# Keys' and queries' bf16 parts stored once in DRAM, repeated by the load

## The chip, the cores and the metric

The kernel runs on one core of a Trainium2 chip. A core has five engines that work side by side: TensorE (PE; its weight loads are listed as PEld), VectorE (DVE), ScalarE (ACT), GpSimd (POOL) and SyncE (SP), and 16 DMA engines. Every DMA but one of this kernel is issued by SP, one after the other; the row "SPq" of the profile is SP's queue. The metric is the time of one execution on the device in microseconds (us). The kernel before took 918.21 us, the median of three runs (917.14 to 920.17).

## The reference

One transformer block over 2,048 rows of width 512. A condition vector gives six modulation vectors. The rows are normalized and modulated, go through an attention with memory (32 heads of width 16, four segments of 512 rows), and then through a second normalization and a bilinear feed-forward layer of width 1,376.

```python
for s in range(N):
    qs, ks, vs = q[:, :, s], k[:, :, s], v[:, :, s]
    logits = jnp.einsum("bhqd,bhkd->bhqk", qs, ks) * scale + mask
    p = _softmax(logits, axis=-1)
    a_dot = jnp.einsum("bhqk,bhkd->bhqd", p, vs)
    pq = phi(qs)
    num = jnp.einsum("bhld,bhde->bhle", pq, M)
    den = jnp.einsum("bhld,bhd->bhl", pq, z)[..., None] + 1e-6
    o = g * (num / den) + (1.0 - g) * a_dot
    pk = phi(ks)
    M = M + jnp.einsum("bhld,bhle->bhde", pk, vs)
    z = z + jnp.einsum("bhld->bhd", pk)
```

The mask is added to the keys that lie before the query's row in the segment, so only keys from the same row back to the first take part. Softmax is of float32 precision, and the kernel keeps it by splitting numbers into parts.

## The kernel before

**Parts.** A float32 key or query is written as a sum of three bf16 numbers, part 0 the largest and part 2 the smallest. Of the nine products of parts, six are kept: 0·0, 0·1, 1·0, 0·2, 1·1 and 2·0. With heads of width 16, six products make a contraction of 6 x 16 = 96 rows, so one bf16 matmul over 96 partitions gives the logits. For that a key tile `kst` holds the parts of the keys in the order 0, 1, 2, 0, 1, 0 (16 partitions each), and a query tile `qst` those of the queries in the order 0, 0, 0, 1, 1, 2. Two more partitions (96 and 97) hold the negative row maximum in two parts and a row of ones, for the second matmul.

**From the projection to the tiles.** `a_kq` (L636) computes keys or queries of one group: eight heads of one segment (four segments, four groups, 16 in all). The projection lies in PSUM as 128 partitions (width times heads) by 512 rows. ScalarE copies it and rounds it to part 0; GpSimd subtracts; ScalarE rounds to part 1; GpSimd subtracts to part 2 (in the very first group VectorE stands in for GpSimd and for the second rounding). The three parts stand side by side in the tile `q3` (two buffers). Three transfers then write them to a DRAM tile of six slots, `kd` or `qd` (L664 and L667): for keys the slots 0 to 2 from parts 0 to 2, slots 3 and 4 from parts 0 and 1, slot 5 from part 0; for queries part 0 three times, part 1 twice, part 2 once. Each such transfer waits only for the parts it reads.

`load(u)` (L228) brings one unit, four heads of a group, from DRAM: one transfer of 96 partitions by 4 KB for keys and one for queries (L231). There are 32 units; four buffers of each tile.

**The loop.** Iteration v (L936) of 34 has five slots. In them unit v+1 or v+2 runs `q_step` (logits with queries as stationary operand; VectorE takes the row maximum), unit v runs `k_step` (L278; logits with keys as stationary operand, less the maximum, then exp on ScalarE and the causal triangle on GpSimd), and unit v-1 runs `av_step` (probabilities times values) and `t_step` (division, store). After slot 2, `n_step` (L268) of unit v+1 brings its row maxima across the partitions: a transpose on TensorE, a copy to `nt` on VectorE and two transfers of one row of 4 KB into partitions 96 and 97 of `qst` (L276), which `k_step` of the next iteration reads. In slot 1, once the projections of the group are done, `load(v+3)` is issued.

Between these steps the loop fills in other work by a fixed rate (`fill`, L868): projections of the next group and segment, the memory, and later the preparation of the feed-forward layer. The loads of units 0, 1 and 2 stand ahead of the loop (L917, L931 and L932). The order of TensorE's instructions is that of the program text; for the other queues, SP's among them, the framework's scheduler orders the instructions by a timeline of its own. SP executes its queue in order. Eight semaphores tell of landed DMAs; they are given out in turn, so that a DMA of SP also waits until the eighth before it has landed, where that isn't known already.

After the loop the feed-forward layer runs (L1002 on), for which keys and queries are no longer used.

Of the kernel before, what the change touches and what calls it, by code (L numbers as in the profile page):

```python
# [10 lines left out]
BF = mybir.dt.bfloat16  # L11
AF = mybir.ActivationFunctionType
# [5 lines left out]
P = 128  # L18
S, D, H, DH, NSEG, L, F = 2048, 512, 32, 16, 4, 512, 1376
KT = D // P  # L20
NG = 4
HG = 8
# [35 lines left out]
def tile_kernel(ctx, tc, x, wq, wk_, wv, wo, beta, w_gate, w_up, w_down, c, w_mod, out):  # L58
    nc = tc.nc
# [19 lines left out]
    def pin(i):  # L79

        if last_pe[0] is not None:
            tc.add_manual_dep(i.ins, last_pe[0].ins.name, NOSYNC, reason="order")

    def MM(*a, **k):
        return pe(nc.tensor.matmul(*a, **k))  # L85
# [4 lines left out]
    CV, CA = Chain(tc, nc.vector), Chain(tc, nc.scalar)  # L90
    vec, act = Switch(nc.vector), Switch(nc.scalar)
    cst = ctx.enter_context(tc.tile_pool(name="cst", bufs=1))
    wpool = ctx.enter_context(tc.tile_pool(name="wp", bufs=1))
    dram = ctx.enter_context(tc.tile_pool(name="dram", bufs=1, space=DRAM))
# [10 lines left out]
    def bank(name, dt=F32, shape=(P, 512)):  # L105

        nbank[0] += 1
        return pst(shape, btag[nbank[0] % len(btag)], name, dt)
# [20 lines left out]
    be = cst.tile([P, H], F32, name="be")  # L129
    e1 = cst.tile([P, KT], F32, name="e1")  # L130

    qd = [[dram.tile([6, P, L], BF, name=f"qd{s}_{g}") for g in range(NG)] for s in range(NSEG)]
    kd = [[dram.tile([6, P, L], BF, name=f"kd{s}_{g}") for g in range(NG)] for s in range(NSEG)]
    memd = [[dram.tile([P, 4 * HG * DH], F32, name=f"memd{s}_{g}") for g in range(NG)] for s in range(NSEG)]
    od = [dram.tile([4, P, D], F32, name=f"od{s}") for s in range(NSEG)]
    x1d = [[dram.tile([P, D], F32, name=f"x1d{s}_{t}") for t in range(4)] for s in range(NSEG)]
# [76 lines left out]
    HQ = 4  # L213
    NB = 4
    NQ = NSEG * NG * 2
    kst = [ap.tile([98, HQ, L], BF, name=f"kst{i}") for i in range(NB)]
    qst = [ap.tile([98, HQ, L], BF, name=f"qst{i}") for i in range(NB)]
# [9 lines left out]

    def load(u):  # L228
        s, g, j = u // 8, u // 2 % 4, u % 2
        for t, d in ((kst[u % NB], kd), (qst[u % NB], qd)):  # L230
            nc.sync.dma_start(t[0:96].rearrange("p h t -> p (h t)"),  # L231
                              d[s][g].rearrange("r (d h) t -> (r d) (h t)", h=HG)[:, j * HQ * L:(j + 1) * HQ * L])

    nms = {}

# [253 lines left out]
    r0 = [[a[:, j].rearrange("p i c -> p (i c)") for a in wm0] for j in range(2)]  # L489
# [139 lines left out]
    def flush():  # L629

        while later:
            later.pop(0)()
# [3 lines left out]
    def a_kq(s, g, nm):  # L636

        hH, hL = hcur[0]
        ph = phs.setdefault((s, g), {})
        if True:  # L640
            dst = kd if nm == "k" else qd
            ps = bank(f"{nm}ps{s}_{g}")
            n = 0
            for k in range(KT):
                for a, b in ((wH, hH), (wL, hH), (wH, hL)):
                    MM(ps, a[nm, g][:, k, :], b[k], start=n == 0, stop=n == 11)
                    n += 1
                    if n in (3, 6, 9):
                        yield 0.68
            f = pa.tile([P, L], F32, tag="f", name=f"{nm}f{s}_{g}", bufs=2)  # L650
            fast = s == 0 and g == 0
            A, V = (CA, CV) if fast else (act, nc.gpsimd)
            A.activation(f, ps, AF.Copy)
            q3 = pa.tile([P, 3, L], BF, tag="q3", name=f"{nm}3_{s}_{g}", bufs=2)
            r = pa.tile([P, L], F32, tag="qr", name=f"{nm}r_{s}_{g}", bufs=2)
            A.activation(q3[:, 0, :], f, AF.Copy)
            V.tensor_sub(r, f, q3[:, 0, :])

            def rest():
                (CV.tensor_copy if fast else act.copy)(q3[:, 1, :], r)  # L660
                V.tensor_sub(q3[:, 2, :], r, q3[:, 1, :])
                for r0, n, k in ((0, 3, 0), (3, 2, 0), (5, 1, 0)) if nm == "k" else ((0, 1, 3), (3, 1, 2), (5, 1, 1)):
                    if nm == "k":
                        nc.sync.dma_start(dst[s][g][r0:r0 + n].rearrange("r p t -> p r t"), q3[:, 0:n, :])  # L664
                    else:
                        i = 3 - k
                        nc.sync.dma_start(dst[s][g][r0:r0 + k].rearrange("r p t -> p r t"),  # L667
                                          q3[:, i:i + 1, :].to_broadcast([P, k, L]))

            if fast:  # L670
                rest()
            phi = (nm == "k" and s < NSEG - 1) or (nm == "q" and s > 0)
            if phi:
                if fast:
                    yield 0.0
                if nm == "q" and g > 0:
                    yield from drain()
                e = pa.tile([P, L], F32, tag="ph", name=f"ph{nm}{s}_{g}", bufs=3)
                rl = pa.tile([P, L], F32, tag="rl", name=f"rl{nm}{s}_{g}", bufs=1)
                act.activation(rl, f, AF.Relu)  # L680
                act.activation(e, f, AF.Exp)
                ph[nm] = e
            yield 0.68
            if not fast:
                rest()
            if phi:
                later.append(lambda: pin(vec.scalar_tensor_tensor(e, e, 1.0, rl, op0=ALU.min, op1=ALU.add)))
                if fast:
                    flush()
        nkq[s, g] = nkq.get((s, g), 0) + 1  # L690
        if nkq[s, g] == 2:
            done.add((s, g))
# [10 lines left out]
    def drain():  # L703
        while memq:
            w = mem_step()
            if w is not None:
                yield w
# [76 lines left out]
    def fill_a():  # L784
# [5 lines left out]
        for s in range(NSEG):  # L790
# [4 lines left out]
            for g in range(2 if s == 0 else 0, NG):  # L795
# [3 lines left out]
                for w in ws:  # L799
                    next(w)  # L800
                K, Q = a_kq(s, g, "k"), a_kq(s, g, "q")
                if g >= 2 and s + 1 < NSEG:
                    if g == 2:
# [101 lines left out]
    next(lw[2])  # L905
    next(lw[2])
    kq0 = [a_kq(0, 0, "k"), a_kq(0, 0, "q")]
    while next(kq0[0]) != 0.0:
        pass
# [5 lines left out]
    run(kq0[1])  # L915
    run(kq0[0])
    load(0)  # L917
    av = a_v(0)
    for i in range(5):
# [6 lines left out]
    for w in w2:  # L926
        next(w)
    run(a_kq(0, 1, "k"))
    run(a_kq(0, 1, "q"))
    flush()  # L930
    load(1)  # L931
    load(2)  # L932
    btag[:] = ["ms"]
    vec.eng = CV
    share = (0.25, 0.0, 0.25, 0.25, 0.25)
    for v in range(-2, NQ + 1):  # L936
        rate[0] = 5.5
        on, prev = 0 <= v < NQ, 0 <= v - 1 < NQ
        for slot in range(5):
            i = (slot + 3) % 5  # L940
            u = v + 2 if i < 3 else v + 1
# [54 lines left out]
    for s in range(NSEG):  # L996
# [30 lines left out]
        for i in range(NF):  # L1027
            if i + 1 < NF:
                gate_up(i + 1)
            n = ft[i][1]  # L1030
# [47 lines left out]
```

## Time and profile before

| what | value |
|---|---|
| median of three runs | 918.21 us (917.14 to 920.17) |
| the profiled execution | 917.86 us, its span 916.1 us |
| TensorE busy | 877.6 us, 96% of the span |
| VectorE, ScalarE, GpSimd busy | 534.9, 408.3, 315.5 us |
| DMA moved | 109.81 MB; HBM read 67.98 MB, written 40.63 MB |
| DMA queue of SP | 37.7% of 16 engines' span |

The span is the time from the first to the last instruction in the trace. Where the profile lists a group of instructions, the line number is that of the code (L85 is the helper for matmuls), then come engine, operation, and the tiles as "written<-read". A row of SPq shows the issue of a transfer, not its movement. "DMA to landing" is the time from that issue until the semaphore tells that all bytes have arrived. A wait is put down to what ended it last.

### The profile page before, as it was taken

Reading aid. Unit: us, or ns where it says so; the run is one execution under the profiler, and the core shown is the slowest. Engines: PE = TensorE matmul, PEld = TensorE weight load, DVE = VectorE, ACT = ScalarE, POOL = GpSimd, SP = SyncE. Lnnn points to the kernel's source line nnn. Section 1 sums busy time; section 2 is a strip of 40 time slices with the busy share of each in tenths; the row PEclk is TensorE's granted clock in tenths of the full one; section 3 lists DMA queues with packets and bytes.
Section 4 is the critical chain, followed back from the end, with each engine's and each line's share of the span. In section 5 each row is a group of like instructions: output and inputs, shape, how many; then the busy total and the mean of one; then the engine's idle time right before and its main releaser. Section 6 shows DMA issues by size and latency. Waiting matters only on the chain.

```text
span 916.1 us, 14191 instructions
## 1 busy us (share of the span) xinstructions
PE 877.6 (96%) x5083; PEld 623.1 (68%) x5084; DVE 534.9 (58%) x1587; ACT 408.3 (45%) x603; POOL 315.5 (34%) x460
## 2 busy tenths in 40 slices
PE   8988999999999899998998999999999999999998
PEld 4655656556656565565655678887888788878886
DVE  8688877897789977787886326553133213321112
ACT  3647767787577865675546412231112111211111
POOL 4435536565464762666424406540000000000000
PEclk9989999999999999998998999999999999999999
DMA  7773544664455544659551433331101110100011
GB/s 230 223 215 115 186 117 155 205 197 145 134 164 178 179 133 125 198 181 307 169 170 59 139 126 109 110 95 58 46 1 47 47 47 0 47 19 29 1 46 47
DMA packets 86215, 109.81 MB, mean 120 GB/s; under 512 B 9504, under 2 KB 58656, under 8 KB 86144
## 3 DMA queue, kind: packets, MB, share of 16 engines
q1 hardware_dynamic: 86000, 108.89, 37.7%
q8 instruction: 40, 0.66, 0.3%
q14 instruction: 31, 0.25, 0.1%
q10 hardware_dynamic: 144, 0.02, 0.0%
HBM read 67.98 MB, written 40.63 MB: 119 GB/s over the span
## 4 chain that ended last, share of the span: by engine, by line
PE 59%; DVE 5%; ACT 3%; issue 1%; DMA 1%; POOL 0%; DVEq 0%
PE gps L1014 13%; PE acc L1035 13%; PE ups L1014 13%; PE wops L85 4%; PE tb L85 3%; PE k L85 3%; DVE q L39 3%; PE q L85 2%; PE qps L85 1%; PE vps L85 1%; ACT pt L296 1%; PE kps L85 1%; PE ctp L88 1%; PE tr L88 1%; PE up L85 1%
## 5 line engine op out<-in xcount | busy, mean ns | idle before, releaser
L39 DVE CUSTOM_DVE_ANT_0 q<-q,cmask 128x384 f32<-128x384 f32 (+3 forms) x512 | 246.9, 508 | 53.0 <-PE q L85 42.6
L296 ACT ACTIVATE pt<-k 128x1024 f32<-128x1024 f32 x160 | 163.7, 1023 | 77.3 <-PE k L85 75.5
L299 POOL TENSOR_SCALAR_AFFINE_SELECT pt<-pt 128x256 f32<-128x256 f32 (+1 forms) x224 | 99.4, 457 | 174.2 <-ACT pt L296 172.0
L1019 DVE TENSOR_TENSOR gs<-gs,ups 128x512 f32<-128x512 f32 (+1 forms) x44 | 30.2, 687 | 194.9 <-PE ups L1014 194.9
L85 PE MATMUL q<-kst,qst 96*128 96x384 bf16 (+3 forms) x512 | 101.6, 303 | 7.7 <-DVE nm L39 5.5
L85 PE MATMUL k<-qst,kst 98*128 98x384 bf16 (+3 forms) x512 | 98.4, 305 | 10.6 <-ACT pt L296 8.0
L1018 ACT ACTIVATE gs<-gps 128x512 f32<-128x512 f32 (+1 forms) x44 | 26.2, 597 | 146.6 <-PE gps L1014 146.6
L1022 ACT ACTIVATE mH<-gs 128x512 fp32r<-128x512 f32 (+1 forms) x44 | 27.8, 633 | 130.2 <-DVE gs L1019 126.7
L85 PE MATMUL tb<-pt,v 128*32 128x512 f32 (+3 forms) x1024 | 76.7, 440 | 0.0
L85 PEld LDWEIGHTS <-kst 98*128 98x128 bf16 x512 | 38.8, 99 | 53.6 <-issue 44.2
L39 DVE DVE_READ_ACCUMULATOR2_ANT nm<- 128x1 f32 x512 | 72.6, 142 | 0.0
L1014 PE MATMUL gps<-chH,gL 128*128 128x512 f32 (+1 forms) x176 | 69.3, 394 | 0.0
L1014 PE MATMUL gps<-chH,gH 128*128 128x512 f32 (+1 forms) x176 | 69.3, 394 | 0.0
L1014 PE MATMUL ups<-chH,uH 128*128 128x512 f32 (+1 forms) x176 | 69.3, 394 | 0.0
L1035 PE MATMUL acc<-dH,mL 128*128 128x512 f32 (+1 forms) x176 | 69.3, 394 | 0.0
L1035 PE MATMUL acc<-dL,mH 128*128 128x512 f32 (+1 forms) x176 | 69.2, 393 | 0.0
L1014 PE MATMUL gps<-chL,gH 128*128 128x512 f32 (+1 forms) x176 | 69.2, 393 | 0.0
L1014 PE MATMUL ups<-chL,uH 128*128 128x512 f32 (+1 forms) x176 | 69.2, 393 | 0.0
L1014 PE MATMUL ups<-chH,uL 128*128 128x512 f32 (+1 forms) x176 | 69.2, 393 | 0.0
L85 PEld LDWEIGHTS <-qst 96*128 96x128 bf16 x512 | 43.6, 98 | 35.2 <-issue 10.1
L1035 PE MATMUL acc<-dH,mH 128*128 128x512 f32 (+1 forms) x176 | 65.0, 395 | 0.0
L85 PEld LDWEIGHTS tb<-pt,v 128*32 128x32 f32 x1024 | 28.7, 110 | 39.9 <-issue 34.5
(215 smaller groups left out, 1660.7 us busy)
## 6 DMA issues: line engine op xcount, KB each, us to landing
kst<-kd SPq DMA_DIRECT2D x32, 384.0 KB, 4.4
qst<-qd SPq DMA_DIRECT2D x32, 384.0 KB, 5.2
wm<-in_w_mod_dram SPq DMA_DIRECT2D x24, 256.0 KB, 5.4
kd<-k SPq DMA_DIRECT2D x16, 384.0 KB, 4.0
qd<-q SPq DMA_DIRECT2D x16, 384.0 KB, 2.9
x<-in_x_dram SPq DMA_DIRECT2D x16, 256.0 KB, 4.2
kd<-k SPq DMA_DIRECT2D x16, 256.0 KB, 3.2
qd<-q SPq DMA_DIRECT2D x16, 256.0 KB, 3.4
```

The costliest lines, as they stand in the source:

```text
L39: i = getattr(self.eng, name)(*a, **k)
L85: return pe(nc.tensor.matmul(*a, **k))
L88: return pe(nc.tensor.transpose(*a))
L296: act.activation(pt, kp, AF.Exp, scale=0.25)
L299: sels[u, i] = nc.gpsimd.affine_select(w, w, pattern=[[0, w.shape[1]], [1, P]], compare_op=ALU.is_ge, fill=0.0, base=0, channel_multiplier=-1)
L1014: nc.tensor.matmul(ps[0:n], a[:, k, 0:n], b[k], start=j == 0, stop=j == 11)
L1018: act.activation(gs[0:n], pss[0][0:n], AF.Copy)
L1019: vec.tensor_mul(gs[0:n], gs[0:n], pss[1][0:n])
L1022: act.activation(mH[0:n], gs[0:n], AF.Copy)
L1035: nc.tensor.matmul(acc[t], a[0:n, t * P:(t + 1) * P], b[0:n, :], start=i == 0 and j == 0, stop=i == NF - 1 and j == 2)
```

## The change

The DRAM tiles `kd` and `qd` have three slots instead of six. Keys are written in the order 0, 1, 2 and queries in the order 2, 1, 0 by one transfer each, once all three parts are there. The repetition moves to the load: each side of a unit is filled by three transfers of 48, 32 and 16 partitions. For keys these read the first 48, 32 and 16 rows of the DRAM tile (parts 0 1 2, 0 1 and 0); for queries the last 48, 32 and 16 rows (parts 2 1 0, 1 0 and 0). The pairs that meet in the contraction are now 0·2, 1·1, 2·0, 0·1, 1·0 and 0·0: the same six products in another order. Per group there are 2 writes and 12 load transfers, where there were 6 and 4.

```diff
-    qd = [[dram.tile([6, P, L], BF, name=f"qd{s}_{g}") for g in range(NG)] for s in range(NSEG)]
-    kd = [[dram.tile([6, P, L], BF, name=f"kd{s}_{g}") for g in range(NG)] for s in range(NSEG)]
+    qd = [[dram.tile([3, P, L], BF, name=f"qd{s}_{g}") for g in range(NG)] for s in range(NSEG)]
+    kd = [[dram.tile([3, P, L], BF, name=f"kd{s}_{g}") for g in range(NG)] for s in range(NSEG)]
...
     def load(u):
         s, g, j = u // 8, u // 2 % 4, u % 2
-        for t, d in ((kst[u % NB], kd), (qst[u % NB], qd)):
-            nc.sync.dma_start(t[0:96].rearrange("p h t -> p (h t)"),
-                              d[s][g].rearrange("r (d h) t -> (r d) (h t)", h=HG)[:, j * HQ * L:(j + 1) * HQ * L])
+        n = HQ * L
+        for t, d, q in ((kst[u % NB], kd, 0), (qst[u % NB], qd, 1)):
+            d = d[s][g].rearrange("r (d h) t -> (r d) (h t)", h=HG)
+            for r, m in ((0, 48), (48, 32), (80, 16)):
+                i = 48 - m if q else 0
+                nc.sync.dma_start(t[r:r + m].rearrange("p h t -> p (h t)"), d[i:i + m, j * n:(j + 1) * n])
...
-            A.activation(q3[:, 0, :], f, AF.Copy)
-            V.tensor_sub(r, f, q3[:, 0, :])
+            i0, i1, i2 = (0, 1, 2) if nm == "k" else (2, 1, 0)
+            A.activation(q3[:, i0, :], f, AF.Copy)
+            V.tensor_sub(r, f, q3[:, i0, :])
 
             def rest():
-                (CV.tensor_copy if fast else act.copy)(q3[:, 1, :], r)
-                V.tensor_sub(q3[:, 2, :], r, q3[:, 1, :])
-                for r0, n, k in ((0, 3, 0), (3, 2, 0), (5, 1, 0)) if nm == "k" else ((0, 1, 3), (3, 1, 2), (5, 1, 1)):
-                    if nm == "k":
-                        nc.sync.dma_start(dst[s][g][r0:r0 + n].rearrange("r p t -> p r t"), q3[:, 0:n, :])
-                    else:
-                        i = 3 - k
-                        nc.sync.dma_start(dst[s][g][r0:r0 + k].rearrange("r p t -> p r t"),
-                                          q3[:, i:i + 1, :].to_broadcast([P, k, L]))
+                (CV.tensor_copy if fast else act.copy)(q3[:, i1, :], r)
+                V.tensor_sub(q3[:, i2, :], r, q3[:, i1, :])
+                nc.sync.dma_start(dst[s][g].rearrange("r p t -> p r t"), q3)
```

## The prediction

> **What bounds the kernel now.** I read the page first, then the busy time by stage, the waits of TensorE, and at last the DMA queue and the tiles that the change touches.
>
> ```profile
> PE 877.6 (96%) x5083; PEld 623.1 (68%) x5084; DVE 534.9 (58%) x1587; ACT 408.3 (45%) x603; POOL 315.5 (34%) x460
> ...
> q1 hardware_dynamic: 86000, 108.89, 37.7%
> ```
>
> TensorE is busy for 96% of the span and the DMA engines for 38%. A change that only touches transfers can move the end only where TensorE stands still for a transfer. The stages (columns: window, length, busy time and count of each engine, granted clock, DMA share, GB/s) show where transfers are dense:
>
> ```profile
> 41.00:62.00 21.00, 17.19 (x86) 11.26 (x87) 18.16 (x67) 8.34 (x13) 7.46 (x6) 0.97 0.87 265
> 62.00:180.00 118.00, 114.18 (x810) 71.59 (x808) 95.73 (x337) 83.69 (x122) 62.19 (x95) 0.98 0.49 153
> 520.00:916.00 396.00, 390.31 (x1741) 313.67 (x1733) 123.81 (x202) 72.34 (x120) 43.12 (x44) 1.00 0.17 54
> ```
>
> From 41 to 62 us the DMA engines are 87% busy and TensorE is idle for 3.8 of 21 us. From 62 us on they are half busy, and after 520 us, where keys and queries are no longer touched, TensorE has the stage to itself. The waits of TensorE (total, times, longest) name the transfers:
>
> ```profile
> PE k L85 <- DMA qst<-nt: 2.6, 1, 2.6
> ...
> PE q L85 <- DMA qst<-qd: 1.0, 1, 1.0
> ```
>
> Only these two waits, 3.6 us together, hang on the tiles of the change, and both stand in the first 62 us:
>
> ```profile
> 58.18 0.39 PE L85 MATMUL qps<-ahL,wqH 128*128 128x512 f32 x1
> 61.18 1.03 PE L85 MATMUL k<-qst,kst 98*128 98x512 bf16 x2 [2.60 <-DMA qst<-nt]
> ```
>
> **The start, where it counts.** Unit 0's first k matmul (61.18) needs the two small rows of row maxima (L276). What stands ahead of them in the queue:
>
> ```profile
> 45.97 0.32 SPq L231 DMA_DIRECT2D kst<-kd  x1
> 46.38 0.38 SPq L667 DMA_DIRECT2D qd<-q  x1
> 46.81 0.43 SPq L588 DMA_DIRECT2D wrk<-in_wk_dram  x1
> 47.29 0.67 SPq L588 DMA_DIRECT2D wrq<-in_wq_dram  x1
> 48.01 0.98 SPq L464 DMA_DIRECT2D x<-in_x_dram  x2
> 49.30 0.33 SPq L231 DMA_DIRECT2D qst<-qd  x1
> 49.67 0.91 SPq L464 DMA_DIRECT2D x<-in_x_dram  x2
> 50.62 0.65 SPq L231 DMA_DIRECT2D kst<-kd  x1
> 51.32 0.51 SPq L231 DMA_DIRECT2D qst<-qd  x1
> 53.37 1.23 SPq L276 DMA_DIRECT2D qst<-nt  x2
> ```
>
> The landing times of the last three lines, each asked for alone, are 9.2, 9.5 and 7.1 to 7.6 us:
>
> ```profile
> DMA to landing us min/median/max: 9.2/9.2/9.2
> ...
> DMA to landing us min/median/max: 9.5/9.5/9.5
> ...
> DMA to landing us min/median/max: 7.1/7.4/7.6
> ```
>
> So the key load lands at 50.62 + 9.2 = 59.8, the query load at 60.8, the small rows at about 61.1: a train of transfers that ends at 61 us holds TensorE. Its bytes: four loads of 384 KB, six of 256 KB (weights and x), a 128 KB query write, together 3,200 KB. If its data begin about 0.9 us after the first issue (an estimate from the two ends of it), it runs at 3,200 KB in 13.9 us, 230 KB per us, close to the 252 GB/s of the stretch:
>
> ```profile
> 53.00:61.00 8.00, 5.53 (x29) 3.59 (x27) 7.75 (x30) 4.28 (x8) 4.51 (x4) 0.98 0.92 252
> ```
>
> **The change part by part.** *Writes.* Each group and side wrote 384 + 256 + 128 KB in three transfers and now writes 384 KB in one: 16 groups x 2 sides x 384 KB = 12.6 MB and 64 issues less. The three went out as their parts became ready; the one waits for the last part, which GpSimd makes (VectorE in the first group). For keys the last write was already the full 384 KB one, so nothing is later there; for queries the last was 128 KB. From the sizes:
>
> ```profile
> kd<-k SPq DMA_DIRECT2D x16, 384.0 KB, 4.0
> qd<-q SPq DMA_DIRECT2D x16, 384.0 KB, 2.9
> ...
> kd<-k SPq DMA_DIRECT2D x16, 128.0 KB, 3.3
> qd<-q SPq DMA_DIRECT2D x16, 128.0 KB, 3.8
> ```
>
> the median landing hardly depends on the size (2.9 to 4.0 us against 3.3 to 3.8), so the write costs -0.9 to +0.7 us per group, off the path.
>
> *Loads.* 64 transfers of 96 partitions (384 KB) become 192 of 48, 32 and 16 partitions (192, 128, 64 KB): the same bytes, 128 more issues; with the writes 64 more in all. SP spends 0.3 to 0.65 us on one (rows above), 0.4 taken: 2 x 0.4 = 0.8 us more per load of a side, 64 x 0.4 = 26 us more on SP over 460 us. What takes the cover in the long stage is time: load(v+3) goes out in slot 1 of one iteration and is used in slot 2 of the next. An iteration is 124.67 - 111.46 = 13.2 us by the issues of the small rows:
>
> ```profile
> 111.46 1.15 SPq L276 DMA_DIRECT2D qst<-nt  x2
> ...
> 124.67 1.15 SPq L276 DMA_DIRECT2D qst<-nt  x2
> ```
>
> ```profile
> kst<-kd SPq DMA_DIRECT2D x32, 384.0 KB, 4.4
> qst<-qd SPq DMA_DIRECT2D x32, 384.0 KB, 5.2
> ...
> qst<-nt SPq DMA_DIRECT2D x64, 4.0 KB, 1.7
> ```
>
> ```profile
> 118.08 0.61 PE L85 MATMUL k<-qst,kst 98*128 98x512 bf16 x2
> ```
>
> A load that lands after 5.2 us has over 8 us to spare; 2 x 0.8 us do not reach TensorE. I take 0; if the loads used up all of that, each further us would be paid in up to 30 units. Behind the loads on SP stand the small rows: issued at 111.46 + 1.15, landed 1.7 us later, used at 118.08, they have some 4 us to spare. SP gives each DMA one of eight semaphores in turn, so a DMA also waits until the eighth before it has landed; a unit's six loads fill most of these. In an iteration the loads leave in slot 1 and the small rows after slot 2, so I take 0 here too.
>
> *Reads of the loaded tiles.* In the changed program's instruction list TensorE, VectorE, ScalarE and GpSimd have the same instructions in the same order; only SP's queue differs. TensorE's first q matmul of a unit waits for three transfers a side, 83 waits more in all. [...] ScalarE and GpSimd wait for one write instead of three before a buffer of parts is used again: 0 to a gain.
>
> *The sum at the start.* Keys' last part of group 1 was issued at 40.74 and landed 5.2 us later behind two other key writes and two query writes; alone I take 3.0 (the 384 KB write of group 0 at 27.1 us):
>
> ```profile
> DMA to landing us min/median/max: 3.0/3.0/3.0
> ...
> DMA to landing us min/median/max: 5.2/5.2/5.2
> ```
>
> ```profile
> 43.73 1.17 POOL L661 TENSOR_TENSOR q<-qr,q 128x512 bf16<-128x512 f32 x1 [1.92 <-ACT q L660]
> ```
>
> So the train starts at 43.7 rather than 45.97, the query write at 44.9 rather than 46.38, with 256 KB more in it: 3,456 / 230 = 15.0 us from 44.6 on, to 59.6, and the small rows at 59.8, 1.4 us earlier. SP's 12 load issues in the train instead of four and the wait for the eighth before take back some; 0.4 taken. The first q matmul (1.0 us of waiting now) moves by -1.0 to +0.6: the query write is three times as large, the load three issues long, the traffic beside it less. It is swallowed by the later wait, since TensorE waits at 58.6 anyway. **Sum: -1.0 us.** The gain ends at -3.6, where both waits are gone. On the other side stands the train slowed by its smaller loads, below.
>
> **The trace's own time** is 917.86 us (span 916.1 and 1.8 around it), 0.35 below the median 918.21. 917.86 - 1.0 = 916.9; against the median 917.2 us.
>
> [...]
>
> **Rivals.** *1, slower: narrow loads move at half speed.* Place: the train. Its last two 384 KB loads land 1.0 us apart (59.8, 60.8), so a side would take 1.0 us more; four sides make +4.0: small rows at 60.2 + 4.0 = 64.2, 3.0 after the 61.2 of before: 921.2. It turns to a loss of over 0.3% from 0.95 us per side on. For it: three transfers share what one had; against: neighbouring transfers overlap in the queue, and 252 GB/s is well below the 314 that the writes reach at 41 to 46 us:
>
> ```profile
> 41.00:46.00 5.00, 4.66 (x22) 3.14 (x23) 3.85 (x15) 1.10 (x2) 1.99 (x2) 1.00 0.90 314
> ```
>
> *2, faster: the writes' time comes back in full* and both waits vanish: 918.2 - 3.6 = 914.6. Against it: the loads, weights and x in the train stay as they are.
>
> *3, slower: SP becomes the bound.* The small rows stand behind six loads and the wait for the eighth before; once they are 4 us late, every further 0.3 us costs 30 x 0.3 = 9 us: 927. The only unit with no room to spare now is that at 281.37, where the rows follow a query load that waited for its write:
>
> ```profile
> 280.96 0.32 SPq L231 DMA_DIRECT2D qst<-qd  x1
> 281.37 1.15 SPq L276 DMA_DIRECT2D qst<-nt  x2
> ```
>
> There two issues more cost 0.8 and the shorter writes give about as much.
>
> [...]
>
> **Chances.** Forecast, within 0.3% (2.75 us, about what a measurement of this kernel can tell from no change): 0.56. Rival 2: 0.17, all of the faster side. Rival 1: 0.18, rival 3: 0.05, rival 4: 0.04, together 0.27 slower. The forecast's own range is 915.5 to 920. Left out at either end are half of rival 2 and the far part of 1 and 3: 914.3 to 921.8.
>
> **What would show it.** Right: HBM bytes written 12.6 MB less, 513 SP issues; the k matmul of unit 0 at 60 us, its wait for the small rows 1.5 to 2.5 us; no other wait for kst or qst above 1 us; landing medians of the loads' three parts of 2 to 5 us. Wrong: a k wait that grows over 4 us (rival 1), TensorE waiting for small rows in many units (3), or gaps ahead of each unit's first q weight load (4).

## The result and the profile after

The changed kernel takes 915.36 us (median of 8 runs, 911.61 to 918.14); the kernel before took 917.67 us beside it (8 runs, 915.25 to 921.4). The ratio is 0.9959, 95% interval 0.9941 to 0.9976: faster by 0.4%. A repetition on another chip (below) gave 0.9977 (0.9961 to 0.9993). The mean over all 21 runs of the changed kernel is 915.60 us, that over 134 runs of the kernel before, made beside the experiments, 918.36 us: 2.8 us less. The prediction had 1.0 us less, too little to be told from no change, as the likeliest.

The profiled execution took 913.71 us (span 912.0). The page of the changed kernel, its parts 1 and 3:

```profile
PE 873.6 (96%) x5083; PEld 622.6 (68%) x5084; DVE 531.9 (58%) x1587; ACT 408.3 (45%) x603; POOL 316.9 (35%) x460
...
q1 hardware_dynamic: 74736, 96.31, 35.8%
...
HBM read 67.98 MB, written 28.05 MB: 105 GB/s over the span
```

The same instructions on every engine, and 12.6 MB less written (40.63 MB before). The list of DMA issues (count, KB each, median us to landing) has the new transfers:

```profile
kd<-k SPq DMA_DIRECT2D x16, 384.0 KB, 3.3
kst<-kd SPq DMA_DIRECT2D x32, 192.0 KB, 3.2
qd<-q SPq DMA_DIRECT2D x16, 384.0 KB, 3.2
qst<-qd SPq DMA_DIRECT2D x32, 192.0 KB, 3.9
...
kst<-kd SPq DMA_DIRECT2D x32, 128.0 KB, 3.4
qst<-qd SPq DMA_DIRECT2D x32, 128.0 KB, 3.9
```

The waits of TensorE, and two stretches of the busy time by stage:

```profile
PE k L85 <- DMA qst<-nt: 2.0, 1, 2.0
...
PE q L85 <- DMA qst<-qd: 0.8, 1, 0.8
```

```profile
41.00:62.00 21.00, 18.05 (x98) 12.38 (x98) 18.86 (x70) 9.21 (x15) 7.50 (x6) 1.00 0.74 206
62.00:180.00 118.00, 112.84 (x813) 70.34 (x812) 97.13 (x346) 84.12 (x124) 64.14 (x100) 1.00 0.45 125
```

The two waits on the tiles of the change stand where they stood, shorter by 0.8 us together; no other wait on `kst` or `qst` has come up. The start in SP's queue, and the k matmul that it leads to:

```profile
43.33 0.77 SPq L235 DMA_DIRECT2D kst<-kd  x2
44.70 0.38 SPq L666 DMA_DIRECT2D qd<-q  x1
45.13 0.47 SPq L235 DMA_DIRECT2D kst<-kd  x1
45.66 0.55 SPq L591 DMA_DIRECT2D wrk<-in_wk_dram  x1
46.25 0.59 SPq L591 DMA_DIRECT2D wrq<-in_wq_dram  x1
46.89 0.50 SPq L467 DMA_DIRECT2D x<-in_x_dram  x1
47.56 1.26 SPq L235 DMA_DIRECT2D qst<-qd  x3
48.86 1.37 SPq L467 DMA_DIRECT2D x<-in_x_dram  x3
50.28 2.95 SPq L235 DMA_DIRECT2D kst<-kd  x3
53.46 2.04 SPq L235 DMA_DIRECT2D qst<-qd  x3
56.95 1.70 SPq L279 DMA_DIRECT2D qst<-nt  x2
```

```profile
60.30 0.60 PE L85 MATMUL k<-qst,kst 98*128 98x512 bf16 x2 [1.98 <-DMA qst<-nt]
```

SP issues the first key load of group 1 at 43.33 instead of 45.97 us, the query write at 44.70 instead of 46.38, and the query load behind it at 47.56 instead of 49.30. The small rows leave later (56.95 instead of 53.37: SP issues unit 3's six transfers first, from 50.28 to 55.5), but land 0.9 us earlier, and unit 0's first k matmul runs at 60.30 instead of 61.18.

Before and now the key load of unit 2 goes out as soon as the last key write of its group has landed. Before, that write was issued at 40.74 and landed after 5.2 us (shown in the prediction); now it is issued at 40.79 and lands after 2.5 us:

```profile
DMA to landing us min/median/max: 2.5/2.5/2.5
```

From unit 0's first k matmul to unit 4's the two profiles move apart by 1.4 us more: 115.81 against 118.08.

```profile
115.81 0.61 PE L85 MATMUL k<-qst,kst 98*128 98x512 bf16 x2
```

Between the first k matmuls of unit 4 and unit 22 nothing moves (252.2 us in the one, 252.1 in the other). The rest of the 4.15 us between these two executions comes and goes near 425 and 500 us, where the granted clock drops to one half for 3.4 or 6.8 us at a time. So there were three candidates for the gain: the start, the granted clock, and the long stage.

### The profile page after: what moved, and what is told of

Its sections match the earlier page's. It is cut to its first block, busy times and chain, and to the rows that moved or that the text cites. A ratio compares the mean times of both kernels' runs of the same rounds, so it can differ in the third digit from the quotient of the medians.

```text
span 912.0 us, 14192 instructions
## 1 busy us (share of the span) xinstructions
PE 873.6 (96%) x5083; PEld 622.6 (68%) x5084; DVE 531.9 (58%) x1587; ACT 408.3 (45%) x603; POOL 316.9 (35%) x460
## 4 chain that ended last, share of the span: by engine, by line
PE 58%; DVE 5%; ACT 3%; POOL 1%; issue 1%; DMA 1%; SPq 0%; DVEq 0%; ACTq 0%
PE gps L1012 13%; PE acc L1033 13%; PE ups L1012 13%; PE wops L85 4%; PE k L85 3%; PE tb L85 3%; DVE q L39 2%; PE q L85 2%; PE qps L85 1%; ACT pt L299 1%; PE vps L85 1%; PE ctp L88 1%; PE up L85 1%; PE tr L88 1%; PE op L88 0%
```

## The experiments

In the expectations stand letters for theories: A, the start, and with it fewer stretches of half clock; B, such stretches fall by chance; C, the long stage; S, the start decides; W, the bytes written; N, the number of writes; Q, the order on SP's queue. Each timed kernel had 8 or 12 runs (the first version with late loads 6), beside runs of the kernel before on the same chip; "ratio" is to these.

### The changed kernel again

> The changed kernel once more. Theory A (the start and the clock): unit 0's small rows land 0.9 us earlier, and because TensorE then idles 2.0 instead of 2.6 us before unit 0's first k matmul, the 6.8 us of half granted clock that followed at 60.7 us before no longer come (worth up to 3.4 us). Then the ratio is 0.995 to 0.997 again, and the granted clock at 60 to 68 us is over 0.95 in this profile too. Rival B (chance): the half-clock stretches fall where they like; the change itself is worth the 0.9 us, ratio 0.998 to 0.9995, and a stretch at 60 to 68 us is as likely here as before. Rival C (the long stage): 12.6 MB less written shortens every unit a little from 62 to 520 us; ratio 0.995 to 0.997 whatever the clock does, and units 1 to 31 come steadily earlier against the profile of before.

Measured: 915.62 us, ratio 0.9977 (0.9961 to 0.9993). Its profile shows an execution of 919.73 us, the slowest of its twelve, with unit 0's first k matmul at 62.31 us, a half-clock stretch of 6.8 us ahead of it (17.5) and another just behind it (begun at 61.8). Another profile of each kernel, taken later, adds to this:

> The changed kernel once more, one profile. Theory S: small rows landed at 60 to 61 us (62.3 in one earlier profile, with 6.8 us of half clock at 17.5), the k matmul within 0.2 us of it, and a half-clock stretch behind it only if the wait is over 2.4 us; unit 4's first k matmul at 115.5 to 117 us without one, near 119 with one.

> The kernel before once more, one profile. Theory S (the small rows' landing sets the start): unit 0's first k matmul stands within 0.2 us of their landing at 61 to 62.5 us. Clock: if TensorE's wait ahead of it is over 2.4 us, a half-clock stretch follows between 60 and 65 us; if it is under 1.5 us, none does. Rival B (chance): stretches without regard to the waits.

> The kernel before once more, one profile: unit 0's first k matmul at the landing of the small rows, 61 to 63.6 us; unit 4's at 118 to 119.2 us, 2 to 2.5 us later than in the changed kernel's profile with the same half-clock stretch near 15 to 24 us.

The start of the second profile of before, SP's queue and the k matmul:

```profile
47.75 0.32 SPq L231 DMA_DIRECT2D kst<-kd  x1
48.16 0.38 SPq L667 DMA_DIRECT2D qd<-q  x1
...
49.07 0.68 SPq L588 DMA_DIRECT2D wrq<-in_wq_dram  x1
...
51.43 0.33 SPq L231 DMA_DIRECT2D qst<-qd  x1
```

```profile
63.54 0.60 PE L85 MATMUL k<-qst,kst 98*128 98x512 bf16 x2 [2.93 <-DMA qst<-nt]
```

The same of the changed kernel's third profile:

```profile
44.78 0.77 SPq L235 DMA_DIRECT2D kst<-kd  x2
46.17 0.38 SPq L666 DMA_DIRECT2D qd<-q  x1
...
47.72 0.64 SPq L591 DMA_DIRECT2D wrq<-in_wq_dram  x1
...
49.34 1.26 SPq L235 DMA_DIRECT2D qst<-qd  x3
```

```profile
61.04 0.60 PE L85 MATMUL k<-qst,kst 98*128 98x512 bf16 x2 [1.24 <-DMA qst<-nt]
```

Both executions have 10.2 us of half clock near 14 us, so they can be laid side by side: key load 3.0 us earlier, query write 2.0, query load 2.1, k matmul of unit 0 2.50, and unit 4's first k matmul also 2.50 (119.06 to 116.56). The three profiles of each kernel:

```
                      wait q  wait k   unit 0's k   unit 4's k
before                  1.0     2.6       61.18       118.08
before, second          1.8     2.9       63.54       119.06
before, third           2.6     1.7       62.97       118.50
changed                 0.8     2.0       60.30       115.81
changed, second         1.1     2.5       62.31       119.22
changed, third          0.8     1.2       61.04       116.56
```

On the mean the two waits fall from 4.2 to 2.8 us, and unit 4 comes 1.35 us earlier (118.55 to 117.20). The key write ahead of all this landed after 5.2, 5.7 and 5.9 us before and after 2.5 us in each profile of the changed kernel.

The spans of these six profiles differ by 2.7 us on the mean, about as the times do. Half of that is the 1.35 us at unit 4; from there to unit 22 all six agree within 0.15 us; the other 1.4 us stand behind unit 22, where stretches of half clock fall near 425 and from 489 to 506 us. Over all twenty profiles of this document the part from unit 22 to the end takes between 542.5 and 549.2 us. Its mean is 545.3 us in the ten of kernels that write half as much there and 546.4 in the other ten: a difference too small to be told from this scatter.

What does not differ is the mean clock: it is 0.9884 over the 134 runs of before and 0.9886 over the 21 of the changed kernel. So theory A's second half isn't borne out: a stretch behind the wait made the first pair of profiles differ by 1.4 us, but one came in one of three profiles of either kernel. Nor does the bound of 2.4 us hold that the expectation set: the second profile of before waited 2.93 us and had no stretch. One row for it (busy times, then granted clock, DMA share, GB/s), of before's first profile and then of its second:

```profile
57.00:76.00 19.00, 15.97 (x78) 10.46 (x77) 15.41 (x52) 11.22 (x18) 8.55 (x16) 0.82 0.44 139
```

```profile
57.00:76.00 19.00, 14.45 (x82) 9.64 (x81) 16.65 (x54) 11.78 (x19) 9.29 (x17) 1.00 0.50 149
```

### The start alone, and all but the start

```diff
+    new = lambda s, g: s == 0 and g < 2          # the other kernel: s > 0 or g > 1
...
-            for r, m in ((0, 48), (48, 32), (80, 16)):
+            for r, m in ((0, 48), (48, 32), (80, 16)) if new(s, g) else ((0, 96),):
```

The DRAM tiles and the writes follow the same condition.

> The change made in groups 0 and 1 of segment 0 alone (units 0 to 3, all that is written and loaded ahead of unit 0's first k matmul); every later group writes its parts as six and loads in one transfer a side, as before. Theory S (the start decides): the whole gain is here, 2.0 to 2.7 us below before, ratio 0.997 to 0.998, and unit 0's first k matmul at 60 to 61 us when no half-clock stretch falls before it. Rival C (the long stage): within 0.7 us of before.

Measured: 916.34 us, ratio 0.9977 (0.9964 to 0.9989).

> The complement: groups 0 and 1 of segment 0 as before, every later group with the change. Theory S: within 0.7 us of before, and the start as in the profile of before (unit 0's first k matmul at 61.2 us plus what half-clock stretches cost). Rival C: 1.5 to 2.5 us below before, with the units from 4 on shorter.

Measured: 917.99 us, ratio 0.9991 (0.9978 to 1.0004). The start alone gives as much as the whole change gave in its repetition (0.9977) and over half of what it gave at first (0.9959); the rest alone, 14 of 16 groups, cannot be told from nothing. The two profiles fit: unit 0's first k matmul at 60.88 and 62.09 us, unit 4's at 116.41 and 118.32. A part of the gain of up to 2 us in the long stage (the low end of that interval) isn't excluded by the times, but up to unit 22 no profile shows it, and behind it the scatter hides so much.

### The loads split, the writes as before

```diff
-            nc.sync.dma_start(t[0:96]..., d[s][g]...[:, j * HQ * L:(j + 1) * HQ * L])
+            for r, m in ((0, 48), (48, 32), (80, 16)):
+                nc.sync.dma_start(t[r:r + m]..., w[r:r + m, j * HQ * L:(j + 1) * HQ * L])
```

> The kernel before with its six written parts a side, and only the loads cut into 48, 32 and 16 partitions (128 transfers more, no byte less). Theory A: nothing gets earlier at the start, the small rows of unit 0 land at 61 to 62.5 us, TensorE waits 2.6 to 4 us for them, time 0 to 2 us above before. The prediction's rival 1 (narrow loads at half speed): small rows at 64, time +3 to +4 us. Rival C (long stage, by bytes written): as before, within 1 us. If the split itself brings the gain: 2 us below before.

Measured: 919.23 us, ratio 1.002 (1.0002 to 1.0037). Small rows at 63.7 us, TensorE's waits 2.2 and 1.7 us. The time is as A has it, but the small rows are not: 63.7 us is outside its 61 to 62.5 and next to rival 1's 64. What made them late is seen below, where the same loads in another order bring them to 59.2 us.

### The write traffic of the start restored

```diff
                 V.tensor_sub(q3[:, i2, :], r, q3[:, i1, :])
+                if s == 0 and g < 2:
+                    nc.sync.dma_start(xd[2 * g + (nm == "q")].rearrange("r p t -> p r t"), q3)
                 nc.sync.dma_start(dst[s][g].rearrange("r p t -> p r t"), q3)
```

> The changed kernel with one more 384 KB write of the three parts, to DRAM that nobody reads, ahead of the write proper in groups 0 and 1 of segment 0 for both sides: the write traffic of the start is what it was before (768 KB per group and side), that of the long stage stays halved. Theory A: the gain is made at the start, so it goes: unit 0's first k matmul is back at 61 to 62.5 us, and the time is within 1 us of before (ratio 0.999 to 1.002). Rival C (long stage): the gain stays, ratio 0.996 to 0.9975. Rival B: 1 us above the changed kernel.

Measured: 918.31 us, ratio 1.0005 (0.9992 to 1.0019): four more writes of 384 KB at the start undo the whole gain. Small rows at 64.6 us. This speaks for the start and against C. The key write of group 1, now behind an extra one, lands after 4.9 us again (issued at 41.42). It doesn't say whether the bytes or the places in the queue did it: SP issued the query load of unit 2 at 51.7 us here.

### The same bytes in three writes

```diff
-                nc.sync.dma_start(dst[s][g].rearrange("r p t -> p r t"), q3)
+                for i in (i0, i1, i2):
+                    nc.sync.dma_start(dst[s][g][i], q3[:, i, :])
```

> The changed kernel with the three parts written by three 128 KB transfers, each as its part becomes ready, instead of one of 384 KB: the bytes of the changed kernel, the issues of the one before. If bytes make the gain: within 0.7 us of the changed kernel (915 to 916.3 us). If the one write matters because it takes fewer places on SP and fewer waits: 1 us or more above it. If waiting for the last part costs something: 0.7 us or more below it.

Measured: 919.11 us, ratio 1.0018 (0.9999 to 1.0038). Not a byte more than in the changed kernel, and the whole gain is gone. So fewer bytes alone do not make it. The start in this kernel's timeline:

```profile
46.41 0.32 SPq L235 DMA_DIRECT2D kst<-kd  x1
...
47.75 0.37 SPq L667 DMA_DIRECT2D qd<-q  x1
48.25 0.82 SPq L235 DMA_DIRECT2D kst<-kd  x2
49.11 0.43 SPq L667 DMA_DIRECT2D qd<-q  x1
...
54.01 0.34 SPq L235 DMA_DIRECT2D qst<-qd  x1
54.39 1.84 SPq L467 DMA_DIRECT2D x<-in_x_dram  x4
...
55.84 1.25 ACT L596 ACTIVATE wkH<-wrk 128x512 fp32r<-128x512 f32 x1 [4.79 <-DMA wrk<-in_wk_dram]
```

With a write for each part, the scheduler puts each load part as soon as its own write may have landed, and between them the other side's writes. SP runs its queue in order: a load that waits for its write keeps the next write back, and that write's landing keeps the next load back. The last query write left at 49.11 us (44.70 in the changed kernel), the last part of unit 2's query load at 54.01, the x loads after that (46.89 to 50.2 there). The weights of group 2 came so late that ScalarE waited 4.79 us for them, and TensorE waited 4.15 us before unit 0's first k matmul, at 62.83.

### The order on SP alone

Three kernels keep loads behind writes with a dependency that orders the queue and adds no wait on the chip (in the third the key load leaves at 47.49 us, 0.3 us after SP has issued the query writes ahead of it, from 45.61 to 47.18). In the first two every load stands behind its side's last write, and for units 0 to 3 behind the last query write of the group:

```diff
+                tc.add_manual_dep(w.ins, wrote["q" if u < 4 else "kq"[q], s, g].ins.name, NOSYNC, reason="order")
```

> As the run with the split loads (six written parts a side, loads of 48, 32 and 16 partitions), but with the loads kept behind the last write of their group in SP's queue (for units 0 to 3 behind the last query write), so that no load that waits for a write stands ahead of another write. Theory Q (SP's order: a load that waits for its write holds up the writes and loads behind it): small rows of unit 0 at 61 to 62 us instead of 63.7, time 917 to 918.3 us instead of 919.4. Theory W (bytes written): no better than 919.

Measured: 917.25 us, ratio 0.998 (0.996 to 1.0001); small rows at 59.2 us, with every byte written that was written before:

```profile
59.24 0.60 PE L85 MATMUL k<-qst,kst 98*128 98x512 bf16 x2 [2.29 <-DMA qst<-nt]
```

> As the run with three writes of 128 KB, in the order on SP of the run just described: these two differ only in the bytes written (384 against 768 KB per group and side). Theory Q: the gain that the three writes had lost comes back, 915.3 to 916.8 us, small rows at 60 to 61.5 us; bytes are worth the difference to the run just described. Theory W: the same as that run would be against it; Theory N (the number of writes, three places on SP and three landings to wait for): 918 to 919.5 us, as with the three writes unordered.

Measured: 915.62 us, ratio 0.9976 (0.996 to 0.9991); small rows at 60.4 us. The last two query writes leave one behind the other, and the key loads follow them:

```profile
42.53 1.56 SPq L670 DMA_DIRECT2D qd<-q  x2
44.20 1.31 SPq L237 DMA_DIRECT2D kst<-kd  x3
...
60.48 0.78 PE L85 MATMUL k<-qst,kst 98*128 98x512 bf16 x2 [3.09 <-DMA qst<-nt]
```

Order alone moves the split loads from 919.23 to 917.25 us and the three writes from 919.11 to 915.62 us. In order, three writes of 128 KB are as good as the one write of the changed kernel (915.36 and 915.62): theory N falls. The two ordered kernels, which differ in bytes alone, are 1.6 us apart in the median but 0.5 in the mean (916.34 and 915.82), with runs from 911.76 to 920.15: what the bytes are worth stays open, between nothing and some 2 us.

In the kernel before, the third changes only this:

```diff
+            if u in (2, 3):
+                tc.add_manual_dep(i.ins, wrote[0].ins.name, NOSYNC, reason="order")   # group 1's last query write
```

> The kernel before, with unit 2's key load put behind group 1's last query write on SP; bytes, writes and loads unchanged. Theory Q: the query write leaves at 44.9 instead of 46.4 us and the query load of unit 2 at 48 instead of 49.3; the small rows land up to 1.4 us earlier and the time falls by 0.7 to 1.8 us (916.5 to 917.6). Theory W: as before, within 0.5 us.

Measured: 916.66 us, ratio 0.9975 (0.9958 to 0.9993). About what the change gives, without the change: no transfer bigger, smaller or fewer, and the scheduler's queue differs only by unit 2's key load behind the query write and its query load ahead of two x loads. But these twelve runs also had the better clock, 0.9903 on the mean where the runs of before beside them had 0.9877. Within the runs of one kernel the time grows by about 0.5 us per us of clock lost (a straight line through the 134 runs of before has 0.55), so by this estimate some 1.3 of the 2.0 us in the mean go with the clock; whether the order or chance brought it is not shown. The comparisons of the first two kernels do not hang on it: the ordered ones ran at 0.9877 and 0.9867, the unordered ones at 0.9862 both, and by the same estimate 2.5 and 3.4 us are left for the order. Its profile does not show the middle of the path: it caught the slowest of the twelve executions (920.91 us, half clock for 6.8 us at 17 and 3.4 us at 44.6), and there the small rows landed at 62.4 us. What it does show is that the query load left at 48.95 us, where the three profiles of before had 49.30, 51.43 and 50.17.

### What else holds the start

Two kernels take bytes from ahead of the small rows. One is before with segment 1's x loads behind them:

```diff
-                        xts[s + 1] = xload(s + 1)
-                        lns = a_ln(s + 1)
+                        lns = late_ln(s + 1) if s == 0 else a_ln(s + 1)   # late_ln issues the x loads a step later
```

> The kernel before, with segment 1's four x loads (256 KB each, 1,024 KB) issued behind unit 0's small rows and so out of the train; at 230 KB/us that is 4.4 us less ahead of the small rows. Theory A: TensorE's wait for unit 0's small rows (2.6 us) is gone or under 0.5 us, k at 58.6 to 59 us; the time falls by 2.1 to 2.6 us, and by up to 3.4 us more if no half-clock stretch follows: ratio 0.994 to 0.9975. Rival B (chance): 2.1 to 2.6 us, clock as before. Against both: if the late x makes the layer norms late, a wait on x shows and the gain is lost (ratio 1.0).

Measured: 919.44 us, ratio 1.0016 (0.9999 to 1.0032). The wait is gone (unit 0's k matmul at 58.49 us), and the time is no better: unit 4 runs at 118.13, as before (118.08). TensorE waits 1.72 us for VectorE's row maxima at 60.8, 1.24 and 1.08 us for x near 84 us (1.13 once in before). A wait had been taken away, and the next one stood behind it. The other puts unit 3's loads, first used at 80.7 us, behind the small rows, in the kernel before and in the changed one:

```diff
+                if u == 3:
+                    pin(w)
```

> The kernel before, with unit 3's two loads (384 KB each, issued at 50.6 and 51.3 us, first used near 88 us) put behind unit 0's small rows. If the small rows wait for the train's bytes, they land 768 / 230 = 3.3 us earlier, at 57.7 us: TensorE's wait of 2.6 us before unit 0's first k matmul is gone or under 0.4 us, and the time falls by 2.0 to 3.0 us (ratio 0.9965 to 0.998). Rival: units 0 to 2 are bound by ScalarE and GpSimd anyway, as with the late x, and less than 1 us of it arrives at the end (ratio 0.999 to 1.001).

Measured: 917.21 us, ratio 0.9985 (0.9973 to 0.9997). In its profile no wait for the small rows is left, but they landed at 60.6 us, not at 57.7, with 10.2 us of half clock ahead of them, and unit 4 starts at 118.25 as before.

> The changed kernel with unit 3's six loads put behind unit 0's small rows. If both gains come from the same wait, the k matmul of unit 0 has no wait left (under 0.4 us instead of 2.0), and the time lies 1.5 to 2.2 us below the changed kernel, 913.3 to 914.1 us, ratio to before 0.9945 to 0.996. Rival (units 0 to 2 bound by other engines): within 0.7 us of the changed kernel.

Measured: 914.34 us, ratio 0.9946 (0.9924 to 0.9967). Once more:

> The changed kernel with unit 3's loads late, once more, for more runs of it beside the one with both edits: 913.5 to 914.8 us, ratio to before 0.994 to 0.997, no wait of TensorE for unit 0's small rows in the profile.

Measured: 915.08 us, ratio 0.9955 (0.994 to 0.997). The wait for the small rows is gone, and in the second run's profile unit 4 starts 1.2 us earlier than in the best profile of the changed kernel (114.61 against 115.81):

```profile
58.04 0.61 PE L85 MATMUL k<-qst,kst 98*128 98x512 bf16 x2
```

Against the kernel before this is the largest gain of all (4.1 and 3.8 us by the medians); against the changed kernel its 14 runs have a mean of 914.5 us where the changed kernel's 21 have 915.6, which the scatter of single runs does not quite tell apart. With the order of the queue added:

```diff
+                if u < 3:
+                    tc.add_manual_dep(w.ins, wrote[g].ins.name, NOSYNC, reason="order")
```

> The changed kernel with both edits of SP's queue: key loads of units 0 to 2 behind their group's query write, and unit 3's loads behind unit 0's small rows. Theory Q: with one write a side little is left that stands in a load's way, so the order adds at most the first q matmul's wait (0.8 to 1.1 us), and the time is 913 to 914.3 us, 0 to 1 us below the version with unit 3's loads late alone. If order and bytes ahead of the rows are independent gains: 1.5 us or more below it, 912.5 us or less.

Measured: 918.29 us, ratio 0.9997 (0.9982 to 1.0013): the gain is lost. Both expected outcomes had it faster. The waits of its timeline say where it went:

```profile
49.11 0.43 SPq L597 DMA_DIRECT2D wrq<-in_wq_dram  x1
...
55.23 1.20 ACT L602 ACTIVATE wqH<-wrq 128x512 fp32r<-128x512 f32 x1 [3.48 <-DMA wrq<-in_wq_dram]
...
58.60 1.20 DVE L39 SCALAR_TENSOR_TENSOR phk<-phk,rlk 128x512 f32<-128x512 f32 x1 [2.44 <-ACT phk L687]
...
62.37 0.59 PE L85 MATMUL q<-kst,qst 96*128 96x256 bf16 x2 [3.56 <-DVE nm L39]
```

The new order has put the query weights of group 2 behind the query load (issue 49.11 instead of 46.17 us). ScalarE stands 3.48 us at their rounding, `phk` behind it is late, VectorE's queue is held by the instruction that waits for `phk`, the row maxima behind that are late, and TensorE waits 3.56 us: a wait for a DMA has become a wait for VectorE.

### TensorE kept busy in the wait

```diff
+        if u == 0 and i == 0:
+            for _ in range(6):
+                MM(kp[:, 0], identb, cmask, start=True, stop=True)
```

> The kernel before, with six dummy matmuls (128x512 bf16, result thrown away) in front of unit 0's first k matmul, so that TensorE idles some 1.3 us less while it waits for the small rows; no transfer changes. Clock theory: where the wait was 2.6 us no half-clock stretch follows at 60 us, units 0 and 1 are 1.4 us shorter, and the time falls by 0.5 to 1.4 us (ratio 0.9985 to 0.9995). Rival B (chance, or the stretch costs nothing): the same time, or up to 1.3 us more where the wait had been short.

Measured: 916.53 us, ratio 0.9982 (0.9961 to 1.0002), with a mean granted clock of 0.9889 (the other kernels have 0.9862 to 0.9903). The time is as the clock theory has it, but the interval reaches past no change and the clock is that of the runs of before beside it (0.9887), so the runs do not settle it; its profile has the wait still at 2.30 us and a half-clock stretch of 3.4 us behind it. Whether filling the wait is worth anything stays open.

## Why the prediction was wrong

**The bound.** Right as far as the profiles go: the change touches TensorE only through the two waits in the first 62 us. The experiments place at least most of the gain there.

**Writes.** The cost of "-0.9 to +0.7 us per group, off the path" is borne out: landing 3.3 and 3.2 us, no unit late. What was not seen is that the write which the first key load waits for lands more than twice as fast; see below.

**Loads.** Right, with 3.2 to 3.9 us per part where one transfer took 4.4 and 5.2; rival 1 (narrow loads at half speed) does not show. Its half was a supposition, and no run shows it: the parts of 48 partitions landed after 3.2 and 3.9 us in the median, and in the ordered kernel with split loads and six written parts the small rows came at 59.2 us, not at 64; that kernel isn't slower than the kernel before (917.25 us, ratio 0.998).

**Rival 3.** SP's wait for earlier transfers showed at the start: three waits for x loads, 3.4 us together, at unit 3's loads and the small rows (later the loads waited six times for other tiles' transfers, 0.4 us at most). SP needed from 50.28 to 55.5 us for unit 3's six loads, and the small rows left 3.6 us later than before, but landed earlier. In no later unit did TensorE wait for them. **Rival 4** (TensorE's 83 extra waits cost time): no run shows such a cost; the 252.2 us from unit 4 to unit 22, against 252.1 before, leave no room for it. **Rival 2** named a time near the result (914.6) but not its mechanism: both waits are still there.

**The step that failed is the sum at the start, -1.0 us.** For the pair of executions it was reckoned on it holds: small rows and k matmul 0.9 us earlier, predicted 1.0. But it was worked out in one execution of before, and that was the one with the earliest start of three: 61.18 us, the others 62.97 and 63.54. It was also the only one of the six without half clock between 8 and 46 us; the others had 3.4 to 10.2 us of it there. In the pair with the same clock at the start the gain is 2.5 us, on the mean of three profiles each 1.35, and in the times 2.3 to 2.8. The terms of the sum, one by one:

- *When the train starts* was mis-sized: "43.7 rather than 45.97", 2.3 us earlier. The key load leaves when the key write has landed. The landing was taken to fall from 5.2 to 3.0 us; it fell from 5.2, 5.7 and 5.9 to 2.5 us each time. So the first key load leaves 2.6 us earlier on the mean (46.8 to 44.2) and 3.0 in the pair with the same clock. (Ahead of that write in the queue stood two key writes, one query write and two loads, not two query writes.)
- *How long the train takes*: its bytes, "3,456 / 230 = 15.0 us", and 0.4 us for SP's issues took back 1.3 us. From the first key load to the landing of the small rows it takes 15.2, 15.7 and 16.3 us before and 16.9, 17.8 and 16.2 in the changed kernel: 1.2 us longer on the mean, as taken, but only 0.5 in the pair with the same clock.
- *The first q matmul* "moves by -1.0 to +0.6" and "is swallowed by the later wait": right. It moved by -0.2 us in the first pair and by -0.8 in the second, and in all six profiles unit 0's k matmul starts within 0.1 us of the landing of the small rows.

What the sum did not have is the order on SP. The same bytes in another order cost 3.5 us (three writes, 919.11 against 915.62), and with every byte kept, order gave the split loads 2.0 us (919.23 against 917.25). In the kernel before, a key load that waits for the last key write stands ahead of the last query write (45.97, 46.38), and everything behind it is late by that. The changed kernel does not undo this order: two parts of the key load still stand ahead of the query write (43.33, 44.70). What it shortens is the landing that they wait for. That the landing is shorter because fewer writes stand ahead of it fits the kernel with the extra writes (4.9 us and no gain), but is argued, not shown by itself.

The chance for "faster" was put on the waits vanishing altogether; a case in which both get shorter by about a third was not among the cases.

**What stays open.** The profiles account for 1.35 us of the 2.3 to 2.8 by the start, and 1.35 alone would still have been within what the forecast called no change. The rest may be scatter of three profiles each, or a part of up to 2 us in the long stage, which the kernel without the start leaves possible. What the bytes are worth by themselves is not settled either.

## What to carry to other kernels

Where one engine issues every DMA in order, look at the queue before the bytes: a load that waits for a write holds back every transfer behind it (in the kernel before, the query write whose last part was ready at 44.90 us left at 46.38, behind the key load of 45.97), so put writes that are ready ahead of loads that still wait, and check what such a move pushes back in turn. Before pricing a start of which one profile is at hand, ask how far it moves from run to run; here by 2.4 us, as much as the effect. And a wait taken from TensorE is worth no more than the room until the next engine's wait: 2.6 us taken away gave nothing in one version, and 3.6 us came back in another.

## What the runs showed of the hardware

The granted clock drops to one half for 3.4, 6.8 or 10.2 us at a time, most often at 14 to 25, 42 to 48, 60 to 69, 421 to 434 and 486 to 509 us in these profiles: in the first of before at 60.7 (6.8 us), 425.9 (6.8), 490.8 (3.4) and 501.0 (3.4), in the first of the changed kernel at 19.0 (3.4), 421.8 (6.8) and 496.9 (3.4). The same kernel gets other ones in each execution: in its first eight runs the changed kernel took from 911.61 us (mean clock 0.995) to 918.14 (0.984). It often follows stretches in which TensorE idles, but not each time: behind a wait of 2.60 us came 6.8 us of half clock, behind one of 2.93 none, behind one of 3.09 3.4 us, behind four waits of 1.2 to 2.0 us none, and behind a fifth of 1.7 us (split loads) again 3.4. What sets them off is not shown. A good part of the scatter of 7 us against which a change of 2.5 us had to be told goes with it, at about 0.5 us per us of clock lost.

The other: the small rows have 4 KB each time, and their landing differed all the same. At the start they took 7.1 to 7.6 us from issue to landing in the first profile of before, 2.1 to 3.1 us in that of the changed kernel; the median of all 64 is 1.7 us in both. That it goes with what stands ahead of them in the queue is argued, not shown by itself.
